# Keeping the split expert weights in DRAM across three passes

## The chip, the cores and the metric

One Trainium2 chip, one of its cores. The metric is the device time of one execution in microseconds; lower is better. Three runs of the kernel before took 2052.97, 2057.09 and 2062.87 us; their median, 2057.09 us, is the time before.

## The reference

Three layers in a row, all in 32-bit floats, on 2304 tokens of width 512:

```
attention: 4 batches, 8 heads, 576 positions, head size 64, causal by blocks of 64
x = attention output, (2304, 512)
P = exp(x @ w_gate - max); eight rounds of dividing by row and column sums   # (2304, 8)
for e in range(8):
    h = maximum(x @ w1[e], 0)            # (2304, 1024)
    out += P[:, e:e+1] * (h @ w2[e])     # (2304, 512)
h = out @ w_in; softmax, h * softmax, layer norm with g_ln, @ w_out
```

The change concerns the expert part: `w1` (8, 512, 1024) and `w2` (8, 1024, 512).

## The kernel before, in words

TensorE is fed operands of type `fp32r`, and every operand is split into a high and a low part for accuracy: ScalarE casts the raw value to the high part (line 427) and GpSimd subtracts that from the raw value to get the low part (line 428); `split_weights` holds both lines. A product then takes three matmuls: high by low, high by high, low by high.

Attention and expert 0 come first. The other seven experts are the long middle stage. An expert is cut into two **units** (halves of its 1024 hidden columns), numbered 2 to 15 over experts 1 to 7; the tokens are cut into three **passes** of 768. The loop at line 793 runs over the 42 pairs of pass and unit, pass outermost, so that each unit's weights are used three times, 14 units apart. In this document a unit's number is the loop's `n`, 0 to 41: pass 0 is 0 to 13, pass 1 is 14 to 27, pass 2 is 28 to 41. One turn of the loop does this:

- `first_layer` (line 623): seven products of a Strassen scheme (`PRODUCTS`, "1627543"), each of a weight factor `W[i]` (tags `wa` and `wb`) and a token factor `X[i]`, 84 matmuls of 384 columns (lines 634 to 636). VectorE adds the products up (`u`, `vu`, `v`, line 640), ScalarE takes the ReLU (line 645) and VectorE makes its low part (line 646).
- `left_factors` (line 580) and `second_weights` (line 612) prepare the **next** unit's weights. The first loads four raw tiles of 256 KB (tag `raw`, five buffers in `stg2`), forms the seven factors with four VectorE operations (lines 600, 601, 602, 608) and splits each. The second loads and splits four tiles of `w2`. Every unit of every pass does this again from the raw weights: 8 loads, 11 splits, 4 VectorE operations.
- `decode` (line 437), in units 4 to 35: one half of a tile of the last layer's weights, which arrive as 64-bit words and are made into 32-bit floats by seven or eight VectorE operations, split, and stored to `wdram`. At the end of the kernel `load_decoded` loads them from there.
- `second_layer` (line 673): six output tiles of 12 matmuls each with 512 columns (lines 682 to 684), accumulated by VectorE into `acc` (line 688).

At each pass's start `spread_x` (line 547) makes the seven token factors anew from `xdram`.

Buffers: the pool `wca` (tag `wa`) has seven factor slots, `wcb` (tag `wb`) four, `w2r` six. An even unit takes all its seven factors from `wa`; an odd one takes the first four of its order from `wb` and the last three from `wa`.

All DMAs are issued by SyncE (SP), in order, on one queue. The order of each engine's instructions is not the program's: a scheduler of the framework simulates the program in time and writes down an order for each engine, with the program's order as the priority, and waits are by semaphores. So the second layer of one unit and the first layer of the next are interleaved on TensorE.

Of the kernel before, what the change touches and what calls it, by code (L numbers as in the profile page):

```python
# [7 lines left out]
F32 = mybir.dt.float32  # L8
F32R = mybir.dt.float32r
F16 = mybir.dt.float16  # L10
U32 = mybir.dt.uint32
AF = mybir.ActivationFunctionType
ALU = mybir.AluOpType
# [5 lines left out]
P = 128  # L19
# [5 lines left out]
def build(ctx, tc, qT, kT, v, w_gate, w1, w1s, w2, w_in, w_out, g_ln, out):  # L25
    nc = tc.nc
# [11 lines left out]
    stg = xctx.enter_context(tc.tile_pool(name="stg", bufs=2, side="left"))  # L38
    dram = ctx.enter_context(tc.tile_pool(name="dram", bufs=1, space=bass.MemoryType.DRAM))
# [6 lines left out]
    class Ring:  # L46
# [6 lines left out]
        def take(self):  # L53
            self.n += 1
            return self.tiles[(self.n - 1) % len(self.tiles)]

    def pool_copy(o, i):
        nc.gpsimd.tensor_scalar(o, i, 1.0, 1.0, op0=ALU.mult, op1=ALU.mult)

    def r32(ap):  # L60
        return ap.bitcast(F32)
# [20 lines left out]
    xlate = [xp.tile([P, 4, 64], F32R, name=f"x{s}late") for s in "hl"]  # L82
    xdram = dram.tile([P, 4, N], F32, name="xd")
    wdram = dram.tile([16, P, 2, 512], F32, name="wd")

# [76 lines left out]
    class Tile:  # L164
# [140 lines left out]
        def split(self):  # L305
            part = self.part()
            if part is None or self.n % 2 == 0:
                return
            b, h = divmod(self.n, H)
            c = h // 2  # L310

            if h == H - 1:
                a, z = ((0, 256), (256, S))[part]
            elif part == 1:
                a, z = 0, S
            else:
                return

            if b % 2 == 0:
                cuts = [(a, min(z, 512), xseg[0], 0), (max(a, 512), z, xlate, -512)]  # L320
            else:
                cuts = [(a, z, xseg[1], 64)]
                if c == 0:
                    for s in range(2):
                        pool_copy(xseg[1][s][:, :, 0:64], r32(xlate[s]))
            nc.sync.dma_start(xdram[:, c, b * S + a : b * S + z], sums[0][:, a:z])
            for a, z, to, off in cuts:
                if z <= a:
                    continue
                x = sums[0][:, a:z]  # L330
                hi, lo = (y[:, c, a + off : z + off] for y in to)
                nc.scalar.copy(hi, x)
                nc.gpsimd.tensor_tensor(lo, x, r32(hi), op=ALU.subtract)
# [92 lines left out]
    def split_weights(t, raw):  # L426
        nc.scalar.copy(t[:, 0, :], raw)  # L427
        nc.gpsimd.tensor_tensor(t[:, 1, :], raw, r32(t[:, 0, :]), op=ALU.subtract)  # L428
# [7 lines left out]

    def decode(i, half, src, scale=None):

        raw = stg.tile([P, 512], F32, tag="raw", name="raw64").bitcast(U32)
        nc.sync.dma_start(raw, src)  # L440
        raw = raw.rearrange("p (n w) -> p n w", w=2)
        lo, hi = raw[:, :, 0], raw[:, :, 1]
        a = dec.tile([P, 256], U32, tag="a64", name="a64")
        b = dec.tile([P, 256], U32, tag="b64", name="b64")
        nc.vector.tensor_scalar(
            a, hi, 3, 0x3FFFFFFF, op0=ALU.logical_shift_left, op1=ALU.bitwise_and
        )
        nc.vector.scalar_tensor_tensor(
            a, hi, 0xC0000000, a, op0=ALU.bitwise_and, op1=ALU.bitwise_or
        )  # L450
        nc.vector.scalar_tensor_tensor(
            a, lo, 29, a, op0=ALU.logical_shift_right, op1=ALU.bitwise_or
        )
        nc.vector.tensor_scalar(
            b, lo, 28, 1, op0=ALU.logical_shift_right, op1=ALU.bitwise_and
        )
        nc.vector.tensor_tensor(a, a, b, op=ALU.add)

        nc.vector.tensor_scalar(
            b, hi, 1, 28, op0=ALU.logical_shift_left, op1=ALU.logical_shift_right  # L460
        )
        f = dec.tile([P, 256], F32, tag="f64", name="f64")
        nc.vector.scalar_tensor_tensor(f, b, 7.0, r32(a), op0=ALU.is_ge, op1=ALU.mult)
        if scale is not None:
            nc.vector.tensor_scalar_mul(f, f, scale)
        t = dec.tile([P, 2, 256], F32R, tag="w64", name="w64")
        split_weights(t, f)
        nc.sync.dma_start(wdram[i, :, :, half * 256 : half * 256 + 256], r32(t))

# [29 lines left out]
    def run(job):  # L499
        for _ in job:  # L500
            pass
# [43 lines left out]
    PRODUCTS = "1627543"  # L545
# [31 lines left out]
            split("3", kc, b22)  # L577
            yield

    def left_factors(u, stg):  # L580

        e, g = divmod(u, 2)
        pools = {i: (wca, "wa") for i in PRODUCTS}
        if u % 2:
            pools.update({i: (wcb, "wb") for i in PRODUCTS[:4]})
        raw = {}
        for i, k in ((1, 1), (2, 1), (2, 2), (1, 2)):
            raw[i, k] = stg.tile([P, 512], F32, tag="raw", name="raw")
            nc.sync.dma_start(raw[i, k], w1s[e - 1, g, i - 1, k - 1])
        a11, a12, a21, a22 = raw[1, 1], raw[1, 2], raw[2, 1], raw[2, 2]  # L590
        W = {}

        def split(i, a):
            pool, tag = pools[i]
            W[i] = pool.tile([P, 2, 512], F32R, tag=tag, name=f"W{tag}")
            split_weights(W[i], a)

        s1 = stg.tile([P, 512], F32, tag="s1", name="s1", bufs=1)
        split("1", a11)
        nc.vector.tensor_tensor(s1, a21, a22, op=ALU.add)  # L600
        nc.vector.tensor_tensor(a21, a11, a21, op=ALU.subtract)
        nc.vector.tensor_tensor(a11, s1, a11, op=ALU.subtract)
        split("6", a11)
        split("2", a12)
        split("7", a21)
        split("5", s1)
        split("4", a22)
        nc.vector.tensor_tensor(a12, a12, a11, op=ALU.subtract)
        split("3", a12)
        return {i: t.rearrange("p s (k f) -> p s k f", k=2) for i, t in W.items()}  # L610

    def second_weights(u):
        e, g = divmod(u, 2)
        ws = []
        for c in range(4):
            r = stg.tile([P, 512], F32, tag="raw", name="raw")
            nc.sync.dma_start(r, w2[e, (4 * g + c) * P : (4 * g + c + 1) * P, :])
            t = w2r.tile([P, 2, 512], F32R, tag="w2", name="w2")
            split_weights(t, r)
            ws.append(t)  # L620
        return ws

    def first_layer(W, X):

# [4 lines left out]
        def product(i, ps, g, start, stop):  # L629
            w, x = W[i], X[i]  # L630
            for kc in range(2):
                wh, wl = (w[:, s, kc, g * P : g * P + P] for s in range(2))
                xh, xl = (x[:, s, kc, :] for s in range(2))
                nc.tensor.matmul(ps, wh, xl, start=start and kc == 0, stop=False, skip_group_check=True)  # L634
                nc.tensor.matmul(ps, wh, xh, start=False, stop=False, skip_group_check=True)  # L635
                nc.tensor.matmul(ps, wl, xh, start=False, stop=stop and kc == 1, skip_group_check=True)  # L636
# [117 lines left out]
    wca = rctx.enter_context(tc.tile_pool(name="wca", bufs=7, side="right"))  # L754
    stg2 = rctx.enter_context(tc.tile_pool(name="stg2", bufs=5, side="right"))
# [5 lines left out]
    W = None  # L761
    for i in range(9):
        next(rounds)
        if i in (1, 5):
            next(spreading)
        if i == 3:
            W = left_factors(2, stg2)
        cost = 0
        while cost < 20:
            cost += next(begun, 20)  # L770
# [5 lines left out]
    dec = ectx.enter_context(tc.tile_pool(name="dec", bufs=1, side="left"))  # L776
    tmpp = ectx.enter_context(tc.tile_pool(name="tmpp", bufs=2, side="left"))
    hp = ectx.enter_context(tc.tile_pool(name="hp2", bufs=9, side="left"))
    stg = stg2

    late = []
    for i in range(16):
        for half in range(2):

            if i < 8:
                a = i % 2 * 1024 + half * 512
                late.append((i, half, w_in[i // 2 * P : i // 2 * P + P, a : a + 512]))
            else:
                c = i - 8
                late.append((i, half, w_out[c * P : c * P + P, half * 512 : half * 512 + 512], gsc[:, c : c + 1]))  # L790
    work = [(p, u) for p in range(3) for u in range(2, 16)]
    nxt = W, second_weights(2)
    for n, (p, u) in enumerate(work):
        W, ws = nxt
        hs = first_layer(W, X)
        if n + 1 < len(work):
            if work[n + 1][0] > p:
                X = {}
                run(spread_x(p + 1, X))
            nxt = left_factors(work[n + 1][1], stg), second_weights(work[n + 1][1])  # L800
        else:
            rctx.close()
            wip = ctx.enter_context(tc.tile_pool(name="wip", bufs=8, side="right"))
            w2p = ctx.enter_context(tc.tile_pool(name="w2p", bufs=8, side="right"))
            wi = [[load_decoded(wip, 2 * dc + f) for f in range(2)] for dc in range(4)]
        if 4 <= n < 36:
            decode(*late[n - 4])
        second_layer(u, p, ws, hs)
    ectx.close()
    lctx.close()  # L810
# [141 lines left out]
```

## Time and profile before

| | |
|---|---|
| median of three runs | 2057.09 us |
| profiled execution | 2058.58 us |
| its span, first to last instruction | 2056.8 us |
| mean granted TensorE clock | 0.988 |
| expert stage, units 0 to 41 | about 459 to 1828 us of the span |
| HBM read / written | 134.76 / 17.83 MB |
| DMA share of 16 engines' span, main queue | 29.5% |

PE is TensorE's matmuls, PEld its weight loads, DVE VectorE, ACT ScalarE, POOL GpSimd, SP SyncE. A row of a group of instructions gives line, engine, operation, output <- inputs, shape and count, then busy time and the mean of one in ns, then the engine's idle time just before them and what ended it. Matmuls overlap in the pipeline, so the sum of their durations exceeds what they cost; the length of a stretch with a known number of matmuls says more.

### The profile page before, as it was taken

What the parts mean: (1) busy time and instruction counts of PE and PEld (TensorE: products, weight loads), DVE (VectorE), ACT (ScalarE), POOL (GpSimd) and SP (SyncE); (2) the same over time, 40 slices, a digit from 0 to 9 for tenths busy, and PEclk for the clock granted to TensorE, in tenths of its full rate; (3) what the DMA queues carried; (4) which work ended last, traced back from release to release, by engine and by line L of the source; (5) the groups of instructions that cost most, each with busy time, mean ns of one, the idle gap of its engine ahead of it and who ended that gap; (6) DMA issues with size and microseconds to landing.
All of it is one profiled execution on the core that took longest, in us unless ns stands there. A gap on an engine that the chain in (4) does not pass through costs nothing.

```text
span 2056.8 us, 29639 instructions
## 1 busy us (share of the span) xinstructions
PE 1959.5 (95%) x10101; PEld 1722.9 (84%) x10101; DVE 1410.2 (69%) x2916; ACT 819.8 (40%) x1801; POOL 969.0 (47%) x890
## 2 busy tenths in 40 slices
PE   5898999799999999999999999999999999999999
PEld 4687988689898888878888888878888889988887
DVE  6867677557576676777676767777677666659774
ACT  5765656424243332433233333433333333324332
POOL 7665645456455444555355444655455444401000
PEclk9999999899999999999999999999999999999999
DMA  8755544222223222322232222322233221140000
GB/s 229 189 152 130 148 128 112 85 61 74 66 87 93 67 86 70 96 88 87 71 94 79 76 77 77 103 72 87 72 93 93 67 77 52 57 164 16 21 21 36
DMA packets 102678, 182.83 MB, mean 89 GB/s; under 512 B 13696, under 2 KB 25984, under 8 KB 102528
## 3 DMA queue, kind: packets, MB, share of 16 engines
q1 hardware_dynamic: 102528, 180.95, 29.5%
q8 instruction: 80, 1.31, 0.2%
q14 instruction: 70, 0.57, 0.1%
HBM read 134.76 MB, written 17.83 MB: 74 GB/s over the span
## 4 chain that ended last, share of the span: by engine, by line
PE 31%; DVE 8%; POOL 7%; DMA 6%; issue 6%; ACT 2%; POOLq 0%; SPq 0%; ACTq 0%; DVEq 0%
PE yps L682 4%; DMA raw<-in_w1s 4%; PE yps L683 4%; PE yps L684 4%; DVE h L646 3%; POOL Wwa L428 2%; POOL w L428 2%; PE ops L888 2%; PE ops L890 2%; PE ops L889 2%; PE h L837 2%; PE h L836 2%; PE h L835 2%; POOL Wwb L428 2%; PE psb L636 1%
## 5 line engine op out<-in xcount | busy, mean ns | idle before, releaser
L682 PE MATMUL yps<-w,h 128*128 128x512 f32 x1008 | 403.0, 400 | 37.5 <-DVE h L646 24.4
L428 POOL TENSOR_TENSOR w<-raw,w 128x512 fp32r<-128x512 f32 x208 | 278.1, 1356 | 270.8 <-ACT w L427 264.4
L683 PE MATMUL yps<-w,h 128*128 128x512 f32 x1008 | 396.3, 393 | 0.0
L684 PE MATMUL yps<-w,h 128*128 128x512 f32 x1008 | 395.1, 393 | 0.0
L428 POOL TENSOR_TENSOR Wwa<-raw,Wwa 128x512 fp32r<-128x512 f32 x168 | 245.5, 1467 | 178.7 <-ACT Wwa L427 158.8
L688 DVE SCALAR_TENSOR_TENSOR acc<-yps,pr,acc 128x512 f32<-128x512 f32 x252 | 183.7, 744 | 179.0 <-PE yps L684 178.9
L682 PEld LDWEIGHTS yps<-w,h 128*128 128x128 f32 x1008 | 190.0, 188 | 84.6 <-DVE h L646 36.0
L684 PEld LDWEIGHTS yps<-w,h 128*128 128x128 f32 x1008 | 190.5, 189 | 41.4
L683 PEld LDWEIGHTS yps<-w,h 128*128 128x128 f32 x1008 | 190.6, 189 | 31.1
L427 ACT CAST w<-raw 128x512 fp32r<-128x512 f32 x208 | 126.0, 617 | 158.7 <-PE yps L684 104.8
L646 DVE SCALAR_TENSOR_TENSOR h<-vu,h 128x384 fp32r<-128x384 f32 x168 | 165.3, 1000 | 29.0 <-ACT h L645 28.7
L427 ACT CAST Wwa<-raw 128x512 fp32r<-128x512 f32 x168 | 101.8, 617 | 199.6 <-DMA raw<-in_w1s 108.8
L428 POOL TENSOR_TENSOR Wwb<-raw,Wwb 128x512 fp32r<-128x512 f32 x84 | 111.1, 1334 | 78.9 <-ACT Wwb L427 71.3
L222 POOL TENSOR_SCALAR e<-e,sv 128x128 f32<-128x128 f32 (+2 forms) x144 | 82.4, 575 | 98.4 <-DVE sv L218 38.7
L872 POOL TENSOR_SCALAR lh<-ln 128x1024 f16<-128x1024 f32 x18 | 18.8, 1043 | 211.2 <-DVE ln L869 116.0
L634 PE MATMUL psb<-X,Wwa 128*128 128x384 f32 x336 | 113.3, 337 | 0.8 <-DVE X L556 0.8
L636 PE MATMUL psb<-X,Wwa 128*128 128x384 f32 x336 | 113.1, 337 | 0.0
L635 PE MATMUL psb<-X,Wwa 128*128 128x384 f32 x336 | 112.9, 336 | 0.0
L636 PE MATMUL psc<-X,Wwa 128*128 128x384 f32 x336 | 112.7, 335 | 0.0
L634 PE MATMUL psc<-X,Wwa 128*128 128x384 f32 x336 | 112.6, 335 | 0.0
L635 PE MATMUL psc<-X,Wwa 128*128 128x384 f32 x336 | 112.5, 335 | 0.0
L645 ACT ACTIVATE h<-vu 128x384 fp32r<-128x384 f32 x168 | 86.1, 521 | 55.3 <-DVE vu L640 55.2
(201 smaller groups left out, 4840.9 us busy)
## 6 DMA issues: line engine op xcount, KB each, us to landing
raw<-in_w SPq DMA_DIRECT2D x208, 256.0 KB, 2.7
raw<-in_w1s SPq DMA_DIRECT2D x168, 256.0 KB, 2.7
kh<-khigh SPq DMA_DIRECT2D x64, 144.0 KB, 2.6
kl<-kraw SPq DMA_DIRECT2D x64, 144.0 KB, 2.7
wd<-w SPq DMA_DIRECT2D x32, 256.0 KB, 2.4
w<-wd SPq DMA_DIRECT2D x16, 512.0 KB, 7.2
vraw<-in_v SPq DMA_DIRECT2D x16, 320.0 KB, 4.2
kraw<-in_kT SPq DMA_DIRECT2D x16, 288.0 KB, 2.9
```

Source lines behind the costliest of these rows:

```text
L222: nc.gpsimd.tensor_scalar(e, e, self.rs, 1.0, op0=ALU.mult, op1=ALU.mult)
L427: nc.scalar.copy(t[:, 0, :], raw)
L428: nc.gpsimd.tensor_tensor(t[:, 1, :], raw, r32(t[:, 0, :]), op=ALU.subtract)
L634: nc.tensor.matmul(ps, wh, xl, start=start and kc == 0, stop=False, skip_group_check=True)
L635: nc.tensor.matmul(ps, wh, xh, start=False, stop=False, skip_group_check=True)
L636: nc.tensor.matmul(ps, wl, xh, start=False, stop=stop and kc == 1, skip_group_check=True)
L645: nc.scalar.activation(h[:, 0], src, AF.Relu)
L646: nc.vector.scalar_tensor_tensor(h[:, 1], src, 0.0, r32(h[:, 0]), op0=ALU.max, op1=ALU.subtract)
L682: nc.tensor.matmul(ps, hl, ws[c][:, 0, :], start=c == 0, stop=False)
L683: nc.tensor.matmul(ps, hh, ws[c][:, 1, :], start=False, stop=False)
L684: nc.tensor.matmul(ps, hh, ws[c][:, 0, :], start=False, stop=c == 3)
L688: nc.vector.scalar_tensor_tensor(a, ps, pr[:, t, e : e + 1], a, op0=ALU.mult, op1=ALU.add)
```

## The change

In pass 0 every split tile is stored to a new DRAM tensor `fd` (14 units, 11 tiles of 512 KB each, 81 MB in all) right after the split. In passes 1 and 2 nothing is loaded raw: `left_factors` and `second_weights` load the seven and four split tiles from `fd` straight into their slots, with no work of ScalarE, GpSimd or VectorE. Decodes move from units 4 to 35 to units 8 to 39. A decode's raw words and its result now share a tile of the tag `wa` (first and second half of a factor slot) instead of a raw tile and a tile of its own.

```diff
+    fdram = dram.tile([14, 11, P, 2, 512], F32, name="fd")
...
     def decode(i, half, src, scale=None):
-        raw = stg.tile([P, 512], F32, tag="raw", name="raw64").bitcast(U32)
+        pair = wca.tile([P, 2, 512], F32R, tag="wa", name="w64")
+        raw = pair[:, 0, :].bitcast(U32)
         nc.sync.dma_start(raw, src)
...
-        t = dec.tile([P, 2, 256], F32R, tag="w64", name="w64")
+        t = pair[:, 1, :].rearrange("p (s n) -> p s n", s=2)
         split_weights(t, f)
...
-    def left_factors(u, stg):
+    def left_factors(u, p, stg):
...
+        def take(i):
+            pool, tag = pools[i]
+            W[i] = pool.tile([P, 2, 512], F32R, tag=tag, name=f"W{tag}")
+            return W[i], fdram[u - 2, int(i) - 1]
+
         def split(i, a):
-            pool, tag = pools[i]
-            W[i] = pool.tile([P, 2, 512], F32R, tag=tag, name=f"W{tag}")
-            split_weights(W[i], a)
+            t, kept = take(i)
+            split_weights(t, a)
+            nc.sync.dma_start(kept, r32(t))
+
+        if p:
+            for i in PRODUCTS:
+                t, kept = take(i)
+                nc.sync.dma_start(r32(t), kept)
+        else:
...
-    def second_weights(u):
+    def second_weights(u, p):
         e, g = divmod(u, 2)
         ws = []
         for c in range(4):
-            r = stg.tile([P, 512], F32, tag="raw", name="raw")
-            nc.sync.dma_start(r, w2[e, (4 * g + c) * P : (4 * g + c + 1) * P, :])
             t = w2r.tile([P, 2, 512], F32R, tag="w2", name="w2")
-            split_weights(t, r)
+            kept = fdram[u - 2, 7 + c]
+            if p:
+                nc.sync.dma_start(r32(t), kept)
+            else:
+                r = stg.tile([P, 512], F32, tag="raw", name="raw")
+                nc.sync.dma_start(r, w2[e, (4 * g + c) * P : (4 * g + c + 1) * P, :])
+                split_weights(t, r)
+                nc.sync.dma_start(kept, r32(t))
             ws.append(t)
...
-        if 4 <= n < 36:
-            decode(*late[n - 4])
+        if 8 <= n < 40:
+            decode(*late[n - 8])
```

The branch behind `else` in `left_factors` holds the raw loads, the four VectorE operations and the seven splits as they were. The callers pass the pass number along.

## Rows read from the trace of the kernel before

**Rows 1.** Page, part 1: busy us (share of the span) xinstructions.

```profile
PE 1959.5 (95%) x10101; PEld 1722.9 (84%) x10101; DVE 1410.2 (69%) x2916; ACT 819.8 (40%) x1801; POOL 969.0 (47%) x890
```

**Rows 2.** Windows: us, PE, PEld, DVE, ACT, POOL busy (x), clock, DMA share, GB/s.

```profile
572.95:666.47 93.52, 93.52 (x469) 84.62 (x468) 62.98 (x100) 34.47 (x67) 50.94 (x38) 1.00 0.29 90
666.47:861.56 195.09, 189.09 (x937) 168.87 (x936) 131.89 (x211) 66.95 (x133) 96.74 (x72) 1.00 0.26 82
861.56:933.52 71.96, 65.03 (x310) 56.61 (x309) 55.50 (x82) 27.70 (x57) 40.94 (x32) 0.98 0.28 87
933.52:1360.47 426.95, 414.20 (x2033) 368.78 (x2032) 295.29 (x470) 147.15 (x292) 206.81 (x156) 0.99 0.26 79
1360.47:1396.89 36.42, 31.71 (x154) 27.38 (x153) 29.51 (x44) 15.01 (x30) 25.48 (x20) 1.00 0.34 112
1396.89:1624.90 228.01, 221.65 (x1097) 197.44 (x1096) 159.60 (x255) 77.78 (x153) 109.70 (x83) 1.00 0.26 79
1624.90:1782.50 157.60, 156.51 (x781) 141.01 (x780) 107.79 (x154) 56.71 (x111) 80.72 (x59) 1.00 0.23 72
```

**Rows 3.** Waits of TensorE and its weight loads: total us, times, longest.

```profile
PEld yps L682 <- DVE h L646: 36.0, 29, 3.1
...
PEld yps L682 <- DVE acc L688: 17.4, 22, 2.9
...
PE yps L682 <- ACT w L427: 2.3, 3, 1.1
```

**Rows 4.** Groups by line: VectorE in the expert stage.

```profile
L646 DVE SCALAR_TENSOR_TENSOR h<-vu,h 128x384 fp32r<-128x384 f32 x168 | 165.3, 1000 | 29.0 <-ACT h L645 28.7
...
L646 DVE SCALAR_TENSOR_TENSOR h<-v,h 128x384 fp32r<-128x384 f32 x84 | 74.5, 887 | 3.1 <-ACT h L645 3.1
...
L608 DVE TENSOR_TENSOR raw<-raw 128x512 f32<-128x512 f32 x42 | 68.3, 1625 | 29.9 <-POOL Wwb L428 28.2 <-POOL Wwa L428 1.6
...
L602 DVE TENSOR_TENSOR raw<-s,raw 128x512 f32<-128x512 f32 x42 | 46.5, 1107 | 2.5
L646 DVE SCALAR_TENSOR_TENSOR h<-psa,h 128x384 fp32r<-128x384 f32 x84 | 46.1, 552 | 74.3 <-ACT h L645 73.9
...
L600 DVE TENSOR_TENSOR s<-raw 128x512 f32<-128x512 f32 x42 | 32.9, 784 | 27.3 <-DMA raw<-in_w1s 23.2 <-POOL w L428 4.1
...
L601 DVE TENSOR_TENSOR raw<-raw 128x512 f32<-128x512 f32 x42 | 30.7, 730 | 1.1
```

**Rows 5.** Timelines of VectorE and GpSimd: start us, us, instruction.

```profile
1101.17 1.64 DVE L646 SCALAR_TENSOR_TENSOR h<-v,h 128x384 fp32r<-128x384 f32 x1
...
1100.80 1.61 POOL L428 TENSOR_TENSOR w<-raw,w 128x512 fp32r<-128x512 f32 x1
```

**Rows 6.** Groups by line: a factor's split on GpSimd and ScalarE.

```profile
L428 POOL TENSOR_TENSOR Wwa<-raw,Wwa 128x512 fp32r<-128x512 f32 x168 | 245.5, 1467 | 178.7 <-ACT Wwa L427 158.8 <-DMA raw<-in_w1s 19.9
...
L427 ACT CAST Wwa<-raw 128x512 fp32r<-128x512 f32 x168 | 101.8, 617 | 199.6 <-DMA raw<-in_w1s 108.8 <-DVE raw L608 43.1 <-DVE raw L602 42.0
```

**Rows 7.** Timeline of SP's queue at the end of the expert stage.

```profile
1812.55 19.19 SPq L472 DMA_DIRECT2D w<-wd  x16
```

**Rows 8.** Line 472, the loads of decoded weights: issue to landing.

```profile
DMA to landing us min/median/max: 3.1/7.2/10.6
```

**Rows 9.** Waits of SP's queue: total us, times, longest.

```profile
SPq L589 <- POOL w L428: 430.8, 84, 27.8
...
SPq L468 <- POOL w L428: 74.5, 32, 4.3
```

**Rows 10.** Lines 468 and 589: issue on SP, ns min/median/max.

```profile
L468 SPq DMA_DIRECT2D wd<-w x32: 518/519/599, 606.1 to 1635.7; - x32
...
L589 SPq DMA_DIRECT2D raw<-in_w1s x168: 327/328/1212, 388.9 to 1764.2; - x168
```

**Rows 11.** Window among the loads of decoded weights; columns as in rows 2.

```profile
1812.00:1822.00 10.00, 9.84 (x44) 7.87 (x44) 4.30 (x8) 1.05 (x2) 0.00 (x0) 1.00 0.84 318
```

More of the change, by code (lines that the diff above doesn't have):

```diff
@@ L585, in left_factors @@
             pools.update({i: (wcb, "wb") for i in PRODUCTS[:4]})
[L586 to L590, printed above, removed]
         W = {}
-        def split(i, a):
+        def take(i):
             pool, tag = pools[i]
             W[i] = pool.tile([P, 2, 512], F32R, tag=tag, name=f"W{tag}")
-            split_weights(W[i], a)
@@ L598, in left_factors @@
[L598 to L609, printed above, removed]
+            return W[i], fdram[u - 2, int(i) - 1]
@@ new lines, in split @@
+        def split(i, a):
+            t, kept = take(i)
[6 more added lines that the diff above has]
+        else:
+            raw = {}
+            for i, k in ((1, 1), (2, 1), (2, 2), (1, 2)):
+                raw[i, k] = stg.tile([P, 512], F32, tag="raw", name="raw")
+                nc.sync.dma_start(raw[i, k], w1s[e - 1, g, i - 1, k - 1])
+            a11, a12, a21, a22 = raw[1, 1], raw[1, 2], raw[2, 1], raw[2, 2]
+            s1 = stg.tile([P, 512], F32, tag="s1", name="s1", bufs=1)
+            split("1", a11)
+            nc.vector.tensor_tensor(s1, a21, a22, op=ALU.add)
+            nc.vector.tensor_tensor(a21, a11, a21, op=ALU.subtract)
+            nc.vector.tensor_tensor(a11, s1, a11, op=ALU.subtract)
+            split("6", a11)
+            split("2", a12)
+            split("7", a21)
+            split("5", s1)
+            split("4", a22)
+            nc.vector.tensor_tensor(a12, a12, a11, op=ALU.subtract)
+            split("3", a12)
@@ L766, in build @@
         if i == 3:
-            W = left_factors(2, stg2)
+            W = left_factors(2, 0, stg2)
         cost = 0
@@ L791, in build @@
     work = [(p, u) for p in range(3) for u in range(2, 16)]
-    nxt = W, second_weights(2)
+    nxt = W, second_weights(2, 0)
     for n, (p, u) in enumerate(work):
@@ L799, in build @@
                 run(spread_x(p + 1, X))
-            nxt = left_factors(work[n + 1][1], stg), second_weights(work[n + 1][1])
+            q, w = work[n + 1]
+            nxt = left_factors(w, q, stg), second_weights(w, q)
         else:
```

## The prediction

> **What bounds the kernel now.** I read the page's busy table first [rows 1]: TensorE 95%, VectorE 69%. TensorE is the bound, but a busy share with modelled matmul ends says little about what is left to win, so I then cut the expert stage into runs of whole units (a unit is half an expert for one pass, 84 matmuls of the first layer and 72 of the second; the cuts stand at a unit's first matmul) and read each run's length [rows 2]. The first row, units 4 to 6, is the yardstick: 93.52 us for 3 units, 31.17 us each, TensorE busy for all of it. Against 31.17 us a unit the others lose:
> - units 7 to 12 (end of pass 0): 195.09 - 6 x 31.17 = 8.1 us
> - units 13 and 14 (the new X of pass 1): 71.96 - 62.34 = 9.6 us
> - units 15 to 27 (pass 1): 426.95 - 13 x 31.17 = 21.7 us
> - unit 28 (the new X of pass 2): 36.42 - 31.17 = 5.3 us
> - units 29 to 35 (pass 2): 228.01 - 7 x 31.17 = 9.8 us
> - units 36 to 40 (pass 2, no decode begun but one left over): 157.60 - 5 x 31.17 = 1.8 us
>
> Together 56.3 us: that is everything that this change can win in the expert stage. The granted clock was 0.98 and 0.99 in two of these rows and 1.00 in the rest, so a few us of the loss are slower matmuls after a stall, and go with the stall.
>
> The waits say who ends the gaps [rows 3]: the second layer's weight loads wait for VectorE, 36.0 us for `h` (L646) and 17.4 us for `acc` (L688); a weight tile ends a gap of TensorE for 2.3 us in all. So VectorE is late at the end of a first layer. Why, two views show. By shape [rows 4], the same L646 takes 552 ns with its source in PSUM (`psa`), but 1000 ns from `vu` and 887 ns from `v`, both in SBUF; L608 is L601's operation with other operands, at 1625 against 730 ns. In time [rows 5], a long one (1.64 us) lies under one of GpSimd's subtractions of the weight split (1.61 us). VectorE's chain of `vu`, `v` and `h`, on which the last second-layer tiles hang, is stretched by GpSimd's split beside it.
>
> **Passes 1 and 2, what goes.** In 28 units the change drops 11 splits each (ScalarE casts, GpSimd subtractions at about 1.4 us [rows 6], some 15 us of GpSimd a unit) and four VectorE operations: 784 + 730 + 1107 + 1625 ns = 4.2 us a unit [rows 4]. GpSimd keeps one subtraction a decode. So L646 should fall to its PSUM price: 4 x (1000 - 552) + 2 x (887 - 552) = 2.5 us a unit more. VectorE's load in pass 1 is 295.29 / 13 = 22.7 us a unit [rows 2]; 22.7 - 4.2 - 2.5 = 16.0 us. The stretch without decodes, units 36 to 40, carries 107.79 / 5 = 21.6 us and loses 0.35 us a unit. The changed passes carry the decodes as well and are still lighter, so 0.35 us is a cautious remainder: the 25 units 15 to 27 and 29 to 40 lose 33.3 us today and 25 x 0.35 = 8.8 us then. **Gain 24.5 us.** Bounds: 33.3 us if nothing stays; nothing if the gaps only change their releaser.
>
> **What comes instead.** Eleven loads of 512 KB a unit in place of eight of 256 KB. The nearest rows are the 16 loads of decoded weights at the end, of the same size, source and queue: SP issued them within 19.19 us [rows 7], and each landed 3.1 to 10.6 us after its issue, 7.2 in the median [rows 8]. At 19.19 / 16 = 1.2 us each, eleven are 13.2 us of a 31.17 us unit: hidden by throughput. By latency: a load starts when the slot's last reader is through, and then takes up to 10.6 us where cast and subtraction took 0.61 + 1.47 us [rows 6] on a raw tile already there. An even unit's last three factors take the slots that the odd unit before it frees at the end of its first layer; behind that lies a second layer: 72 matmuls of 512 columns against 84 of 384 are 53% of a unit's columns, 16.6 us of its 31.17. The two second-layer weights that find no free slot among six have a first layer, 14.6 us, before them. Both covers exceed 10.6 us, so I take 0. If the cover is gone (the order puts the product earlier), every us late in every unit costs 28 us; a gain from the loads themselves is bounded by the 2.3 us that TensorE waits for weights now.
>
> **Decodes.** Their number and operations stay; they leave units 4 to 7 and enter 36 to 39, where they now have no split beside them. In pass 0, units 7 to 12 lose 8.1 / 6 = 1.35 us each, and decoding started in unit 4 shows its first loss in unit 7: starting later frees about one such unit, 1.4 us (bounds 0 and 8.1). The raw words now come into a factor slot (seven of tag `wa`): before an even unit all seven are wanted, so a decode of an odd unit gets its slot only when that even unit's first product is done, and two fall into the same unit. Nobody on TensorE's side waits for a decode before the kernel's end; behind its load on SP only loads for the next unit are queued, which the same covers hide. I take 0; at worst two decodes in one unit bring back the 1.35 us in half the 24 units, 16 us.
>
> **Pass 0, what is added.** 154 stores of 512 KB on the one SP queue, each waiting there for its subtraction, with raw loads queued behind. The nearest row is the decode's store: SP waited 74.5 / 32 = 2.3 us for GpSimd before each [rows 9]. With the issue itself, 0.52 us for a store and 0.33 for a load [rows 10], a unit would in full take SP 11 x (2.3 + 0.52) + 8 x 0.33 = 33.7 us, 2.5 over 31.17: 35 us over 14 units, the upper bound. The lower is 0: no reason for a gain. Mostly SP already waits for the same event, GpSimd freeing a raw tile (430.8 us in 84 waits [rows 9]), so the store shares a wait that exists; I take 0.2 us a unit, 3 us. Traffic of 11 x 0.52 + 8 x 0.26 = 7.9 MB in 31.17 us is 252 GB/s, under the 318 GB/s of ten microseconds among the 16 loads [rows 11].
>
> **Pass borders.** Units 13, 14 and 28 lose 14.9 us while X is spread by ScalarE, VectorE and GpSimd; that work stays, only the next unit's splits leave these engines. I take a third, 5 us (bounds 0 and 14.9).
>
> **Sum.** 24.5 + 1.4 - 3 + 5 = 27.9 us. The profiled execution took 2058.58 us, 1.5 us over the median of the three runs, 2057.09; I subtract from the median: 2029 us. The bounds: all 56.3 won gives 2001; no gain in passes 1 and 2 but the full store cost gives 2092. About 0.5% (10.3 us) is what a measurement of this kernel can tell from no change.
>
> **Rivals.** *As forecast* (0.68): VectorE stops being late, 2010 to 2046 us.
> *The wait changes its name* (0.16): TensorE waits for a load instead. One factor a unit 0.9 us late, 28 x 0.9 = 25 us, gives back the gain: 2054 us. For it: the slots are few and a load takes longer than a split. Against: the covers of 14.6 and 16.6 us.
> *SP's queue becomes the pace of pass 0* (0.13), the one that ends slower. Stores waiting for GpSimd hold raw loads back, splits start late, the next store later still. It decides if SP's waits add to those it has: 35 us instead of 3 in pass 0, and where raw loads and splits alternate instead of overlapping in the five raw tiles, more. With the gain of the later passes halved: 2057 + 35 - 12 - 6 = 2074 us.
> *The loads come one after another* (0.02). At the fastest landing, 3.1 us, eleven are 34.1 us a unit, 2.9 over 31.17: 28 x 2.9 = 82 us, 2111 us. Against it stands the row of 16 loads in 19.19 us [rows 7]. The Trainium skill, page DMA: Bandwidth & Descriptors, section Anatomy of one DMA, gives about 2 us fixed plus the bytes at 436 GB/s (fitted on another issue path); the estimate from that for 512 KB is 3.2 us, 35 us a unit if the fixed part did not overlap.
> *The change does not do what it says* (0.01): the splits dropped are not on the critical units; 2055 us.
>
> **Numbers.** Faster by over 0.5% is the forecast and its good side plus a sliver of the second case, 0.70; within 0.5%, most of the second, 0.15; slower, 0.15. The range 2010 to 2062 leaves out some 5% below (most of the borders won too) and 15% above.
>
> **What the profile would show.** Right: `h<-vu` at about 550 ns in passes 1 and 2, GpSimd nearly idle there, stretches of units 15 to 27 at 31.2 to 31.6 us a unit with every wait on L646 under 1 us, pass 0 unchanged. Wrong: TensorE or its weight loads released by a load of kept weights, SP waits for GpSimd in pass 0 followed by late casts, or units of pass 0 above 33 us.

## The result, and the profile of the changed kernel

The changed kernel takes 2006.99 us in the median of five runs (2005.1 to 2010.55), the one before 2057.09 us (2052.97 to 2063.76, five runs). The ratio is 0.975, with a 95% interval of 0.973 to 0.977: 50 us faster. The forecast was 2029 us with a range from 2010: the right sign, but 28 us of gain where 50 came, and a time 3 us below the range. The profiled execution took 2010.55 us, 48.0 us less than the profiled one before, and is read against that.

First the page's busy table of the changed kernel, which answers to [rows 1]:

```profile
PE 1944.5 (97%) x10101; PEld 1724.0 (86%) x10101; DVE 1229.0 (61%) x2804; ACT 659.7 (33%) x1493; POOL 542.3 (27%) x582
```

GpSimd's busy time fell from 969 to 542 us, VectorE's by 181. TensorE's count of instructions is the same. Where the time went is read from the windows, cut at the first matmul of units 7, 15, 28, 29 and 41 as in [rows 2]; the columns are us, busy of PE, PEld, DVE, ACT and POOL with counts, granted clock, DMA share, GB/s:

```profile
672.65:922.10 249.45, 249.45 (x1246) 225.08 (x1245) 169.60 (x270) 84.48 (x167) 109.72 (x82) 1.00 0.71 262
922.10:1328.50 406.40, 406.40 (x2033) 367.44 (x2033) 213.95 (x420) 75.53 (x154) 11.59 (x15) 1.00 0.59 206
1328.50:1359.69 31.19, 31.19 (x158) 28.22 (x156) 21.16 (x42) 7.72 (x16) 5.42 (x5) 1.00 0.58 210
1359.69:1734.24 374.55, 374.55 (x1874) 338.65 (x1873) 195.29 (x383) 65.94 (x134) 8.84 (x12) 1.00 0.56 199
```

Units 7 to 40 now take 1061.59 us; at the rate of the yardstick (31.17 us a unit) they would take 34 x 31.17 = 1059.8. Before they took 1116.03 us [rows 2]. So 54.4 of the 56.3 us that the prediction had counted as lost are back: the tensor engine is busy in each window from end to end, at a granted clock of 1.00. In the two windows of passes 1 and 2 GpSimd works 12 and 9 us.

The sum closes so: 54.4 us from units 7 to 40 and 1.1 from units 0 to 6, less 0.3 in the tail, less 7.3 because the stage begins later, 466.8 us into the span against 459.5: 48.0 us in all. The row of the first product in the changed kernel (duration min/median/max in ns, first and last start):

```profile
L653 PE MATMUL psa<-X,Wwa x168: 334/337/346, 466.8 to 1722.6; 128*128 128x384 f32 x168
```

I do not count that start as the change's doing: in the experiments below, in which attention was not touched either, the stage begins between 460.1 and 467.9 us, with the changed kernel's stores or without. Why it moves was not tried.

Who ends TensorE's gaps, over units 0 to 40 of the changed kernel (total us, times, longest), answering to [rows 3]: two waits on its weight loads, and none on its matmuls.

```profile
PEld yps L701 <- DVE h L665: 0.5, 2, 0.3
PEld yps L701 <- DVE acc L707: 0.2, 1, 0.2
```

And the groups of VectorE in passes 1 and 2, answering to [rows 4], with what is left of GpSimd's splits there:

```profile
L665 DVE SCALAR_TENSOR_TENSOR h<-vu,h 128x384 fp32r<-128x384 f32 x105 | 57.8, 551 | 4.8 <-ACT h L664 3.4
...
L665 DVE SCALAR_TENSOR_TENSOR h<-v,h 128x384 fp32r<-128x384 f32 x53 | 29.2, 552 | 2.8 <-ACT h L664 2.8
L665 DVE SCALAR_TENSOR_TENSOR h<-psa,h 128x384 fp32r<-128x384 f32 x52 | 29.0, 557 | 27.1 <-ACT h L664 26.6
...
L430 POOL TENSOR_TENSOR w<-f,w 128x256 fp32r<-128x256 f32 x26 | 19.2, 737 | 752.9 <-ACT w L429 714.5 <-PE yps L703 38.3
```

The low parts with two SBUF sources now take what the one with a PSUM source takes, about 552 ns, as the prediction had put it. The price of that, the DMAs (KB each, us from issue to landing in the median) and SP's waits in pass 0:

```profile
Wwa<-fd SPq DMA_DIRECT2D x140, 512.0 KB, 4.3
w<-fd SPq DMA_DIRECT2D x112, 512.0 KB, 5.9
fd<-Wwa SPq DMA_DIRECT2D x70, 512.0 KB, 3.9
fd<-w SPq DMA_DIRECT2D x56, 512.0 KB, 5.2
Wwb<-fd SPq DMA_DIRECT2D x56, 512.0 KB, 3.8
```

```profile
SPq L600 <- POOL Wwa L430: 103.4, 30, 8.9
SPq L638 <- POOL w L430: 74.2, 29, 28.1
SPq L600 <- POOL Wwb L430: 36.7, 20, 3.4
```

The loads land within 3.8 to 5.9 us in the median (10.3 at the longest), and the waits above name none of them. SP does wait for GpSimd at the stores (lines 600 and 638), 214 us in these three rows, 15 us a unit of pass 0, and nobody waits for SP: window 7 to 14 above runs at the full rate.

### The profile page after: what moved, and what is told of

Same layout as the page of the kernel before. It is cut to its first block, busy times and chain, and to the rows that moved or that the text cites. A ratio compares the mean times of both kernels' runs of the same rounds, so it can differ in the third digit from the quotient of the medians.

```text
span 2008.8 us, 28989 instructions
## 1 busy us (share of the span) xinstructions
PE 1944.5 (97%) x10101; PEld 1724.0 (86%) x10101; DVE 1229.0 (61%) x2804; ACT 659.7 (33%) x1493; POOL 542.3 (27%) x582
## 4 chain that ended last, share of the span: by engine, by line
PE 90%; DMA 4%; DVE 2%; issue 1%; POOL 1%; SPq 1%; ACT 1%; DVEq 0%; POOLq 0%; ACTq 0%
PE yps L701 12%; PE yps L703 11%; PE yps L702 11%; PE psb L653 4%; PE psb L654 4%; PE psb L655 4%; PE psa L653 3%; PE psa L655 3%; PE psa L654 3%; PE psc L655 3%; PE psc L653 3%; PE psc L654 3%; PE ops L908 2%; PE av L282 2%; PE ops L910 2%; PE ops L909 2%
## 5 line engine op out<-in xcount | busy, mean ns | idle before, releaser
L701 PE MATMUL yps<-w,h 128*128 128x512 f32 x1008 | 394.7, 393 | 0.2 <-DVE acc L707 0.2
L702 PE MATMUL yps<-w,h 128*128 128x512 f32 x1008 | 394.2, 391 | 0.0
L703 PE MATMUL yps<-w,h 128*128 128x512 f32 x1008 | 391.9, 391 | 0.0
L430 POOL TENSOR_TENSOR w<-f,w 128x256 fp32r<-128x256 f32 x32 | 23.6, 738 | 771.9 <-ACT w L429 733.6
L703 PEld LDWEIGHTS yps<-w,h 128*128 128x128 f32 x1008 | 189.3, 188 | 41.2
L430 POOL TENSOR_TENSOR w<-raw,w 128x512 fp32r<-128x512 f32 x96 | 132.6, 1388 | 56.6 <-ACT w L429 56.1
L659 DVE TENSOR_TENSOR u<-psb,r 128x384 f32<-128x384 f32 x168 | 92.4, 553 | 52.0 <-PE psb L655 48.7
L665 DVE SCALAR_TENSOR_TENSOR h<-vu,h 128x384 fp32r<-128x384 f32 x168 | 114.1, 682 | 12.9 <-ACT h L664 10.6
L659 DVE TENSOR_TENSOR vu<-psc,u 128x384 f32<-128x384 f32 x168 | 92.3, 553 | 38.1 <-PE psc L655 37.5
L664 ACT ACTIVATE h<-psa 128x384 fp32r<-128x384 f32 x84 | 41.0, 491 | 217.2 <-PE psa L655 213.6
L430 POOL TENSOR_TENSOR Wwa<-raw,Wwa 128x512 fp32r<-128x512 f32 x56 | 81.0, 1453 | 74.9 <-ACT Wwa L429 74.9
```

The lines of the kernel that those rows point to most:

```text
L659: nc.vector.tensor_tensor(t, bank[g, a], tmp[g, "r1" if a == "b" else name[1:]], op=ALU.add)
L664: nc.scalar.activation(h[:, 0], src, AF.Relu)
L665: nc.vector.scalar_tensor_tensor(h[:, 1], src, 0.0, r32(h[:, 0]), op0=ALU.max, op1=ALU.subtract)
L701: nc.tensor.matmul(ps, hl, ws[c][:, 0, :], start=c == 0, stop=False)
L702: nc.tensor.matmul(ps, hh, ws[c][:, 1, :], start=False, stop=False)
L703: nc.tensor.matmul(ps, hh, ws[c][:, 0, :], start=False, stop=c == 3)
```

## The experiments

The forecast's mechanism held and its size did not, so the questions are which part of the change carries the gain, and why passes, borders and pass 0 gave back nearly everything. Three theories: GpSimd's reads beside VectorE's two-source operations (1), the decodes' place and raw tile (2), VectorE's four operations (3); a fourth, that the chain of splits makes VectorE late whatever its sources, comes up with the PSUM runs.

To compare kernels I use one number from each trace, called the **loss**: for every matmul of units 0 to 40, the distance from its start to the next matmul's start, less 0.176 us in a first layer or 0.228 us in a second one (the distances in the undisturbed units), added up. It comes from one execution of each kernel. In us:

```
kernel                             u7-12  u13-14  u15-27   u28  u29-40  u0-40
before                               7.9    10.3    20.7   5.9    10.5   57.5
changed                              0.5     0.0     0.1   0.0     0.2    1.9
decodes alone                        5.4     7.9    17.6   6.6    16.9   57.3
kept weights alone                   5.1     4.7     0.0   0.0     0.0   11.4
stores alone                         5.7     9.1    19.6   6.2    12.4   54.2
changed, GpSimd back                 0.6     0.5    16.3   5.7    16.4   40.6
changed, VectorE back                1.7    -0.1    -0.1  -0.1     0.0    2.9
changed, both back                   1.3     3.8    42.3   6.7    41.9   97.3
changed, GpSimd memsets              1.6     2.8     0.2   0.0     0.1    6.5
changed, GpSimd back, PSUM source    0.1     1.5     9.2   3.9     8.4   24.1
before, PSUM source                  4.9     8.4    13.6   5.2     6.6   41.2
changed, decodes in raw tiles        0.5     1.6     2.1   0.0    -0.1    5.3
changed, decodes from unit 4         4.1     0.6     0.1   0.0     0.0    6.1
```

The last column holds 1.3 us in every kernel that are no gap: six matmuls of expert 0's second layer that run in between in unit 0. How far like kernels differ, the first column shows: "GpSimd back", "VectorE back", "both back" and "GpSimd memsets" have the changed kernel's code for units 7 to 12, and lie between 0.6 and 1.7 us there, the changed kernel at 0.5.

**Decodes alone.** The kernel before with the change's decodes and nothing else:

```diff
-        raw = stg.tile([P, 512], F32, tag="raw", name="raw64").bitcast(U32)
+        pair = wca.tile([P, 2, 512], F32R, tag="wa", name="w64")
+        raw = pair[:, 0, :].bitcast(U32)
...
-        t = dec.tile([P, 2, 256], F32R, tag="w64", name="w64")
+        t = pair[:, 1, :].rearrange("p (s n) -> p s n", s=2)
...
-        if 4 <= n < 36:
-            decode(*late[n - 4])
+        if 8 <= n < 40:
+            decode(*late[n - 8])
```

> Only the decodes change: factor slot instead of raw tile, units 8 to 39. Splits stay in all passes. Theory 1 (GpSimd's subtractions stretch VectorE's low parts L646): the 33 us of units 15 to 27 and 29 to 40 stay, h<-vu stays near 1000 ns, total within 10 us of 2057. Theory 2 (a decode's raw tile among the five raw tiles delays the next unit's splits into the end of the first layer): units 7 to 13 lose under 2 us instead of 11.7, and most of the losses of passes 1 and 2 go too, 2015 to 2030 us.

2057.48 us, ratio 0.997 (0.995 to 0.999) to the kernel before, which took 2062.76 us in the median beside it. The waits of TensorE's weight loads are those of [rows 3] over again:

```profile
PEld yps L683 <- DVE h L647: 39.7, 40, 2.9
PEld yps L683 <- DVE acc L689: 15.6, 22, 2.4
```

Theory 2 falls as a cause by itself: pass 0 improves by some us, units 36 to 40 get worse now that they decode, and the stage's loss is unchanged at 57.3.

**Kept weights alone.** The changed kernel with those lines turned back: decodes in raw tiles, from unit 4.

> Weights kept in DRAM as in the change, decodes as before (raw tile, units 4 to 35). Theory 1 (GpSimd beside VectorE): passes 1 and 2 free of loss, pass 0 with 8 to 12 us, total 2015 to 2022 us. Theory 2 (decode's raw tile): passes 1 and 2 free too, since no raw tile is wanted there, but pass 0 keeps its 11.7 us or loses more, since the stores come on top. What tells them apart is pass 0 against the first kernel of this call.

2016.08 us, ratio 0.978 (0.974 to 0.981). From unit 15 on nothing is lost, decodes and all; two places are left, 4.3 us in unit 9 and 4.7 in unit 14. So keeping the weights carries 46.1 of the 55.6 us of loss that went, and the decodes the last 9.5, which by themselves, in the run above, they did not win.

**GpSimd back.** The changed kernel, with the eleven subtractions a unit done again in passes 1 and 2 on the loaded tiles, into a scratch tile:

```diff
+    def again(t):
+        s = stg2.tile([P, 512], F32, tag="s1", name="again", bufs=1)
+        nc.gpsimd.tensor_tensor(s, r32(t[:, 0, :]), r32(t[:, 1, :]), op=ALU.subtract)
...
                 nc.sync.dma_start(r32(t), kept)
+                again(t)
```

> The changed kernel, with GpSimd's eleven subtractions a unit done once more in passes 1 and 2 on the loaded tiles, into a scratch tile that nobody reads. Theory 1 (port): h<-vu rises from about 550 to 850 ns or more, units 15 to 40 lose 15 to 33 us again, 2022 to 2040 us. Theory 3 (the four VectorE operations and the chain behind the raw tiles were the cause): loss under 5 us, 2007 to 2012 us.

2046.07 us, ratio 0.993 (0.991 to 0.996): 38 us over "VectorE back" (the next experiment), which was timed beside it. VectorE's groups in passes 1 and 2 (from 900 us on) and the wait that returns:

```profile
L671 DVE SCALAR_TENSOR_TENSOR h<-vu,h 128x384 fp32r<-128x384 f32 x108 | 111.1, 1042 | 1.4 <-ACT h L670 1.2
L671 DVE SCALAR_TENSOR_TENSOR h<-v,h 128x384 fp32r<-128x384 f32 x54 | 67.2, 1247 | 2.6 <-ACT h L670 2.5
...
L671 DVE SCALAR_TENSOR_TENSOR h<-psa,h 128x384 fp32r<-128x384 f32 x56 | 31.0, 555 | 17.9 <-ACT h L670 17.4
```

```profile
PEld yps L707 <- DVE h L671: 18.7, 17, 1.8
```

No result hangs on these subtractions, ScalarE and the raw loads stay out of it, and yet `h<-vu` is at 1042 ns again while the same line with a PSUM source stays at 555. The loss returns: 38.4 us in units 15 to 40 (the columns u15-27, u28 and u29-40), where the kernel before lost 37.1, with the one at the border of unit 28 (5.7 us) among them. No wait of TensorE or of its weight loads in this stage is for a load of kept weights. This is the run that shows the cause for these units. For units 7 to 12 it can show nothing, since the reads put back begin with unit 14's weights; and in units 13 and 14, the first border, only 0.5 of 10.3 us come back, while unit 15 loses 6.8 us where it lost 1.3.

**VectorE back.** The same with four VectorE operations instead: `nc.vector.tensor_tensor` in `again`, called for the factors "1", "6", "2" and "3" only.

> The changed kernel, with four more VectorE operations a unit in passes 1 and 2 on loaded tiles (128x512, both sources in SBUF) into a scratch tile. Theory 3 (VectorE's load): 15 to 33 us of loss come back. Theory 1: GpSimd is idle, the four cost about 0.7 us each, 2.8 us a unit in VectorE's idle time, loss under 5 us, 2007 to 2012 us.

2008.24 us, ratio 0.973 (0.970 to 0.976), loss 2.9 us. Without GpSimd each takes its short time:

```profile
L586 DVE TENSOR_TENSOR again<-Wwa 128x512 f32<-128x512 f32 x70 | 48.4, 692 | 27.9 <-DMA Wwa<-fd 27.7
L586 DVE TENSOR_TENSOR again<-Wwb 128x512 f32<-128x512 f32 x42 | 30.7, 730 | 0.8
```

Theory 3 falls as a cause by itself: four operations, 2.8 us a unit, cost 1.0 us of loss in all when nothing stretches them.

**Both back.** GpSimd's subtractions and, on a raw tile as scratch, the four VectorE operations:

```diff
+    def add(t):
+        s = stg2.tile([P, 512], F32, tag="raw", name="added")
+        nc.vector.tensor_tensor(s, r32(t[:, 0, :]), r32(t[:, 1, :]), op=ALU.subtract)
...
                 again(t)
+                if i in "1623":
+                    add(t)
```

> The changed kernel with both back in passes 1 and 2: GpSimd's eleven subtractions a unit and four VectorE operations with two SBUF sources, all into scratch. Alone, GpSimd's gave back 38.7 us of loss in the stage and VectorE's four 1.0 us. If the four operations cost only where GpSimd stretches them (each waits for a subtraction), the loss is 45 to 70 us, 2050 us or more. If they are harmless beside GpSimd too, it stays near 41 us, 2043 to 2049 us.

2101.93 us, ratio 1.020 (1.018 to 1.023): slower than the kernel before. The loss is 97.3 us, far above the 38.7 and 1.0 that the two bring alone. The four operations and TensorE's waits:

```profile
L590 DVE TENSOR_TENSOR added<-Wwa 128x512 f32<-128x512 f32 x70 | 75.8, 1083 | 82.6 <-DMA Wwa<-fd 82.6
L590 DVE TENSOR_TENSOR added<-Wwb 128x512 f32<-128x512 f32 x42 | 68.0, 1660 | 0.0
```

```profile
PEld yps L713 <- DVE h L677: 41.0, 25, 4.0
PEld yps L713 <- DVE acc L719: 34.1, 31, 3.8
```

692 ns became 1083 and 730 became 1660. In this kernel all four run as the loads land, beside GpSimd's subtractions on the same tiles, a harder case than the kernel before; but the interplay is plain. These four VectorE operations are all but free beside an idle GpSimd and dear beside a reading one, and what they delay now is `acc` too.

**GpSimd memsets.** In place of each subtraction two memsets of the scratch tile (`nc.gpsimd.memset(s, 0.0)`): GpSimd is busy and reads nothing.

> The changed kernel, with GpSimd kept busy in passes 1 and 2 by 22 memsets a unit of the scratch tile: it writes and reads nothing. Theory 1 in the form that it is GpSimd's reading that VectorE's second SBUF source waits for: h<-vu stays near 550 to 700 ns, loss under 3 us, about 2008 us. In the form that any GpSimd access to SBUF does it: h<-vu 900 ns or more where they overlap, loss of 10 us or more, 2018 us or more.

2010.51 us, ratio 0.975 (0.969 to 0.981). The memsets' group, then a piece of the two timelines (start us, us), then VectorE's groups in passes 1 and 2:

```profile
L587 POOL MEMSET again<- 128x512 f32 x616 | 325.2, 528 | 33.8
```

```profile
1099.68 11.84 POOL L587 MEMSET again<- 128x512 f32 x20
```

```profile
1102.19 0.55 DVE L672 SCALAR_TENSOR_TENSOR h<-vu,h 128x384 fp32r<-128x384 f32 x1
...
1109.12 0.54 DVE L672 SCALAR_TENSOR_TENSOR h<-v,h 128x384 fp32r<-128x384 f32 x1
1110.39 0.54 DVE L672 SCALAR_TENSOR_TENSOR h<-vu,h 128x384 fp32r<-128x384 f32 x1
```

```profile
L672 DVE SCALAR_TENSOR_TENSOR h<-vu,h 128x384 fp32r<-128x384 f32 x112 | 62.2, 555 | 4.3 <-ACT h L671 2.5
```

The low parts in the piece lie wholly under memsets and take 0.54 to 0.55 us. That GpSimd is busy does not stretch them; that it reads does. By the Trainium skill, page SBUF — State Buffer, section Who interferes with whom, a VectorE instruction with two SBUF inputs contends with a GpSimd instruction that reads SBUF and not with one that only writes it; the two runs agree, 1042 against 555 ns.

**PSUM source, before and after.** In the kernel before, the sums `v` and `vu2` stay in their PSUM bank, so that four of a unit's six two-source low parts have one SBUF source; the same edit once more in the kernel "GpSimd back":

```diff
-            t = tmp[g, name] = tmpp.tile([P, BLK], F32, tag=name, name=name)
+            if name in ("v", "vu2"):
+                t = bank[g, a]
+            else:
+                t = tmp[g, name] = tmpp.tile([P, BLK], F32, tag=name, name=name)
```

> The kernel before, every split and decode as it was; only the last two sums of a first layer (v and vu2) are written back into their PSUM bank instead of SBUF, so that four of the six low parts a unit that had two SBUF sources have one. Theory 1 (two SBUF sources wait for GpSimd): h<-v and the vu2 half of h<-vu fall to 552 ns and half or more of the 56 us goes, 2020 to 2040 us. Theory 4 (VectorE is late because of the split chain's waits, whatever the source): no change, 2050 to 2062 us. The banks are held some 2 us longer, which could cost back a few us.

> The changed kernel with GpSimd's eleven subtractions a unit back in passes 1 and 2, and the sums v and vu2 left in their PSUM bank, so that only the vu3 half of the low parts (two a unit) and the decode have two SBUF sources. If the 38.7 us that GpSimd brings back come through the low parts of the last sums, under 12 us of loss are left, 2012 to 2022 us. If they come through vu3 and the decode, or through something else that GpSimd delays (slots, loads), 20 us or more are left, 2028 us or more.

The first takes 2049.51 us, ratio 0.994 (0.992 to 0.996); the second 2031.68 us, 0.987 (0.984 to 0.989). In the first, by shape:

```profile
L649 DVE SCALAR_TENSOR_TENSOR h<-vu,h 128x384 fp32r<-128x384 f32 x84 | 84.7, 1012 | 27.1 <-ACT h L648 27.1
...
L649 DVE SCALAR_TENSOR_TENSOR h<-psb,h 128x384 fp32r<-128x384 f32 x84 | 45.9, 546 | 2.3 <-ACT h L648 2.2
L649 DVE SCALAR_TENSOR_TENSOR h<-psc,h 128x384 fp32r<-128x384 f32 x84 | 45.0, 548 | 7.4 <-ACT h L648 6.9
```

The four fell to 547 ns beside the same splits, and the loss by 16.3 us (57.5 to 41.2) in the one and 16.5 (40.6 to 24.1) in the other. Theory 4 of the first expectation (no change) falls; but theory 1 had put half or more of the loss on these low parts, and 16.3 of 57.5 us went. In the second the expectation's other branch came: 24 us remain.

Counted by unit, the remainder has a place. In "GpSimd back" units 14, 15, 28 and 29, where X is new, lose 18.6 us and the other units of passes 1 and 2 lose 20.3; with the PSUM source it is 20.3 and 2.6. So away from the borders the last low parts carry nearly all of what GpSimd's reads cost there, and at the borders they carry none of it. In the kernel before, the same edit took the units away from the borders from 28.7 us only to 17.9. In the stage's waits of TensorE's weight loads in the second kernel the sums and the copy `r` come first (7.6 of the 8.8 us for `r` at the borders), and `h` is down to 1.5 us:

```profile
PEld psa L659 <- ACT r L686: 8.8, 4, 5.0
PEld psc L659 <- DVE vu L668: 3.1, 1, 3.1
```

What is left to be stretched is `vu3`, the low parts of X (line 560: `X<-b` takes 1069 ns from 1325 to 1375 us, against 632 in the changed kernel) and the decode. The decode is stretched: here are two of its operations in "GpSimd back", from 900 us on, which take 415 (L452) and 352 ns (L449) in the changed kernel:

```profile
L452 DVE SCALAR_TENSOR_TENSOR a<-w,a 128x256 uint32<-128x256 uint32 x26 | 22.7, 873 | 0.0
L449 DVE TENSOR_SCALAR a<-w 128x256 uint32<-128x256 uint32 x26 | 22.2, 853 | 28.9 <-DMA w<-in_w_out 15.9 <-DMA w<-in_w_in 12.9
```

How the border's 20.3 us divide between these was not tried.

**Stores alone.** The kernel before plus the 154 stores (`nc.sync.dma_start(kept, r32(t))` behind each split, `if not p`); the stored tiles are never read.

> The kernel before plus the 154 stores of pass 0 and nothing else; the stored tiles are never read. As the prediction put it: pass 0 loses 3 us more, 35 at most, 2060 to 2092 us. Rival: the stores cost nothing or reorder pass 0 for the better, pass 0 (units 7 to 13) loses 5 us or less instead of 11.7 and passes 1 and 2 their 33 us plus borders as before, 2048 to 2058 us.

2060.6 us, ratio 0.999 (0.997 to 1.001). The loss in units 7 to 12 is 5.7 us, against 7.9; the stores cost nothing that this run can tell. Passes 1 and 2 keep theirs.

**The decode's two moves, one at a time.** The changed kernel with raw tiles again but the late start, and with factor slots but the start in unit 4 (`4 <= n < 36`):

> The changed kernel with the decode's raw words back in a raw tile and its result in a tile of its own; decodes stay in units 8 to 39. If the factor slot matters: unit 14 and some unit of pass 0 lose 4 us each, as with decodes wholly as before, 2015 us. If only the later start matters: under 3 us lost in the stage, about 2008 us.

> The changed kernel with decodes in units 4 to 35 again, still in factor slots. With weights kept and decodes wholly as before the stage lost 11.4 us (unit 9: 4.3, unit 14: 4.7); with the late start but raw tiles 5.3 us. If the start is what matters: 8 to 12 us here, about 2013 us. If the slot is: 2 to 5 us, about 2008 us.

2008.53 us (ratio 0.974, 0.968 to 0.980) and 2013.55 us (0.977, 0.974 to 0.980). The late start takes 4.2 us of loss away (6.1 to 1.9), all of it in pass 0, the factor slot 3.4 us (5.3 to 1.9), around units 14 to 17. The two intervals overlap, so the losses by unit are the only evidence. That of the late start, 3.6 us in units 7 to 12, is above the 1.2 us by which like kernels differ there; that of the slot is not clear of it: "GpSimd memsets", with the slots, loses 2.8 us in units 13 and 14. That the slot matters is likely, not shown.

## Why the prediction was right in its mechanism and wrong in its size

- **What bounds the kernel: right.** TensorE is the bound, its gaps in this stage come to 56 us, and VectorE's low parts, stretched under GpSimd's reads, end them. "GpSimd back" against "memsets" and "VectorE back" shows it three ways for units 15 to 40. One reading was a little too tidy: the long `h` of [rows 5] ends at 1102.81 us, 0.40 us behind the subtraction that it is said to lie under.
- **Passes 1 and 2, the step that failed first.** The 552 ns were right, and VectorE's load of 16.0 us a unit came out at 213.95 / 13 = 16.5. But the remainder of 0.35 us a unit was taken from units 36 to 40, and those still had all eleven splits beside them: a row of the old state served as the floor of the new one. Measured: (406.40 + 374.55 - 25 x 31.17) / 25 = 0.07 us a unit, a gain of 31.6 us where 24.5 stood. The bound named beside it, 33.3, was the better value.
- **Pass borders, the second.** I took a third of 14.9 us because the work on X stays. But the loss was not that work's alone: with the splits gone from beside it unit 28 runs at 31.19 us, and with GpSimd's reads put back it loses 5.7 us again, the work on X being the same. Unit 28 alone gave 5.2 us, and units 13 and 14 nearly all of their 9.6; for these two the reads put back do not show the cause, since 0.5 us came back there and the rest a unit later.
- **Pass 0, the third.** 1.4 us of gain less 3 of cost were forecast. Units 7 to 14 went from 267.05 to 249.45 us, 0.1 over the yardstick, so that, without the 9.6 of units 13 and 14, pass 0 gave some 8 us. The store's price was wrong: SP's waits for GpSimd came, 15 us a unit where 11 x 2.3 = 25 had been the full price, but the raw loads behind them were early enough. "Stores alone" measures no cost. The late start, put at 1.4 us, measured 4.2 in the changed kernel. Splits still run in pass 0, and low parts are still stretched there (`h<-vu` takes 945 ns in the mean from 466 to 900 us), yet no gap follows. Each part alone leaves 4 to 6 us in units 7 to 12, stores and late start together 0.5. The scheduler draws up a new order for each kernel; which of its differences decides there was not settled.
- **The three together.** 31.6 us came where 24.5 stood, some 14.8 where 5 stood and some 8 where 1.4 less 3 stood, 54.4 in place of 27.9; the later start of the stage hid 7.3 us of that in the profiled execution.
- **What comes instead: right.** Eleven loads of 512 KB a unit stayed hidden, at landings of 3.8 to 5.9 us in the median and 10.3 at the longest, against covers of 14.6 and 16.6.
- **Decodes: right that two in one unit are harmless** once GpSimd is idle: each unit of passes 1 and 2 with them is within 0.1 us of the yardstick.
- **The range.** Its low end left out the case that everything comes back, 2001 us, because three terms were each set well inside their bound in the same direction. Two of them were not independent: one cause, GpSimd's reads, stood behind the passes' loss and at least the second border's, and the change takes it away in both.

In this stage hardly a gap is left for a further version: 0.6 us in 41 units, the table's 1.9 less the 1.3 of expert 0's matmuls.

## What to carry to other kernels

When an engine's operation has two durations by the same line and shape, and one depends on what another engine does meanwhile, the gain from removing that other work is bounded by all gaps that the slow duration ends; take the remainder from the undisturbed case, not from the best stretch of the disturbed kernel. Terms that hang on one cause move together, so a range must hold the sum of their far ends. A round trip through DRAM can beat recomputing where the recomputing engine's reads stretch the operations that TensorE waits for and the DMAs have room (a share of 0.3 before, 0.53 after).

## What the runs showed of the hardware that was not expected

- A GpSimd memset of 528 ns leaves VectorE's two-source operation at 555 ns; a GpSimd subtraction of some 1400 ns takes it to 1042. Not every operation was untouched by memsets: the decode's L458 takes 498 ns in the mean beside them, 286 in the changed kernel.
- Delays do not add: GpSimd's reads alone cost 38.7 us, four VectorE operations alone 1.0, both together 95.4 over the changed kernel's 1.9. My reading, not tested further, is that VectorE's idle time here takes up either its own added work or the stretching, not both.
- Stretched beside GpSimd's reads was also a VectorE operation with one SBUF source: L449, a `tensor_scalar` that shifts 128x256 words, 853 ns there against 352. The Trainium skill, page SBUF — State Buffer, section Who interferes with whom, names `tensor_scalar` among the operations that can contend.
- DMA traffic of 262 GB/s in the window of units 7 to 14 (share 0.71), three times the 82 GB/s of before in units 7 to 12 [rows 2], went with no loss on TensorE: it kept the yardstick's rate.
